# Four quarters of the array for state times q, and GpSimd scatters paced by row tile, in a fused retention and two-layer kernel

## The chip, the cores and the metric

The kernel runs on one NeuronCore of one Trainium2 chip. The metric is device time in microseconds (us), lower is better. The engines are called PE (TensorE, with PEld for its weight loads), DVE (VectorE), ACT (ScalarE), POOL (GpSimd) and SP (SyncE, which issues most transfers). A program line is written L331; the line numbers are those of the kernel before unless the text says otherwise.

## The reference, cut to what matters

Three layers follow each other. Attention with decay (retention) over 8 batches, 8 heads, 576 positions, 64 numbers a head:

```python
scores = q @ k.T / 8
Dmat   = gamma[h] ** (i - j) where i >= j, else 0
x      = (scores * Dmat) @ v            # [4608 tokens, 512]
```

Then a mixture of 8 experts, each token going to the one with the largest logit, and a dense layer with a squared relu:

```python
e = argmax(x @ w_gate + modality_bias[modality_id]);  gate = softmax(...)[e]
x = gate * (relu(x @ w1[e]) @ w2[e])
out = relu(x @ w_in) ** 2 @ w_out
```

All of it is computed in 32-bit floats.

## The kernel before, in words

The program has three stages: retention and routing (to about 232 us of the span), experts (to about 700 us), dense layer (to the end). The change touches the first stage alone.

The first stage walks over 36 row tiles of 128 tokens; nine row tiles hold two batches. For row tile `m` the loop issues, in a fixed order that is written out by hand (each engine takes its instructions in that order):

- `state(m)`: keys times values of the tile are added to a running sum `dps` in PSUM (L312), and ACT copies it, scaled, to `st` (L315).
- `keys(m+1)`, `scores(m+1)`: PE transposes the next tile's keys (`pk`, L278) and DVE scales them (`kj`); PE multiplies keys by queries (`pss`, L290) and DVE masks them to `pm` (L294).
- `outp(m)`: the output of the tile. Eight products of the state with q (L331, the "state products") and eight of v with the masked scores (L334) add up in a PSUM tile `po`. DVE multiplies `po` by a table into `xT` (L342), the transposed rows, which has six buffers.
- `rows_out(m-1)`: PE transposes the rows of the tile before (`pt`, L350), ACT copies them to `xr` and SP writes them to memory as `xl`.
- every fourth tile `logits` (L362, four products side by side in column strips of 32), and then some steps of the routing: the tokens of a group of up to 8 row tiles are ranked by DVE, and each tile gets one scatter on POOL (L447) that writes 128 records of 8 bytes to the table `perm`, each to the row that its rank gives. A one-element memset `spacer` (L446) stands ahead of each scatter.

The heads are taken in pairs: `hp` is the pair (0 to 3), `par` the head in the pair. q, keys and state of a pair lie with head `par` 0 on partitions 0 to 63 and `par` 1 on 64 to 127. A state product contracts over the 64 partitions of its head and writes 64 partitions of `po`, the same half: rows 0 to 63 of the array to columns 0 to 63, or rows 64 to 127 to columns 64 to 127. It is absent in the first tile of a batch pair, and has half as many columns in the tile where the batches meet: 32 tiles have it.

`scatter_some(n)` puts up to `n` scatters that are ready into the program at the end of a row tile: 2 up to tile 28, 4 after it, but none in tiles 27 and 28, where eight gathers (L517) go out for an early expert block. A scatter waits for its ranks only; nothing in it refers to the row tile at whose end it stands, so POOL runs through all scatters of a group once the ranks are there. The records are read back by SP later in the first stage and in the second (`rec`, `recr`).

The pool for `po` has two buffers of one PSUM bank each; with the other pools all eight banks are taken.

Of the kernel before, what the change touches and what calls it, by code (L numbers as in the profile page):

```python
# [5 lines left out]
F32 = mybir.dt.float32  # L6
# [6 lines left out]
A = mybir.AluOpType  # L13
# [5 lines left out]
P = 128  # L19
B, H, S, D = 8, 8, 576, 64  # L20
NT = B * S
DM = H * D
E = 8
# [28 lines left out]
def layouts(inputs):  # L52
# [10 lines left out]
    o["wg"] = np.ascontiguousarray(inputs["moe_w_gate"].reshape(4, P, E).transpose(1, 0, 2))  # L63
    o["mb"] = np.ascontiguousarray(inputs["moe_modality_bias"]).reshape(1, 2 * E)
    o["w1"] = np.ascontiguousarray(inputs["moe_w1"].reshape(E, 4, P, 2, 512).transpose(0, 3, 2, 1, 4).reshape(E, 2, P, 2048))
# [7 lines left out]
def consts():  # L73
# [10 lines left out]
    tabi = gh[:, :, None] ** p.astype(np.float64) / 8.0  # L84
# [33 lines left out]
OPT = dict(manual=True, nbig=10,nlate=10,nx=2,b0=2,bl='SG',rl=2,pz=5,ve=lambda m:'GV' if m<3 or m%4==0 else 'GS',vn=(4,4,2),egn=4,nps=2,npo=2,npt=2,npm=4,nwarm=11,ew=(20,25,32,33),es={23:1,24:1,25:1,26:1,28:1,29:1,30:1,31:1},rlag=2,rlagl=1,rlate=35,rperl=30,e5=5,e6=4,ld=4,rper=8,nw=3,biasat=4,keep=(5,0,4,2),nxw=3,scs=9,e3=11,ylag=2,zlag=2,gb=3,zb=4,cf=(0,6,7,12),cf0=(0,8,9,13),hv=10,zend=1,cwm={0:3},cws={i:(1 if i<4 else 2) for i in range(2,14)},cv0=8,scat=lambda i,n: (2 if i<29 else 4),f3=32,f4=33,e0=dict(ro=1,esplit={2:4,3:2,4:2},r1=0,r2=2,r3=2,tab=(5,6,7,8),rec=4,raw=(0,1,2,3),g1=6,split={5:2,6:2,7:2,8:3,9:3,10:2,11:2},xn1=9,tr0=6,tr1=4),hh=3,hl=3,ylag2=1,bs1=dict(regs=1,rec=1,raw=(3,4,5,6),g0=3,g1=7,gn0=(2,)*4,gn1=(2,)*4,split={6:1,7:1,8:2,9:2,10:1,11:2,12:2,13:1,14:2,15:2},tr0=10,tr1=13,cv=1),bs=dict(regs=-9,rec=-9,raw=(0,3,6,8),g0=-4,g1=4,gn0=(1,)*8,gn1=(1,)*8,split={5:1,6:1,7:2,8:2,9:2,10:2,11:2,12:2,13:2},tr0=5,tr1=13,cv=0,f0=7,p0=13,wm={0:1,3:1,7:1,11:1,13:1},ws={3:2,4:2,5:2,6:2,9:2,10:2}))  # L118


def kernel_body(tc, I, out):
# [199 lines left out]
    def outp(m):  # L321

        t = ins[m]
        r = m % PER
        po = ps_o.tile([P, 4, P], F32, name="po")
        n = C if r == PER // 2 else P
        if r:
            for hp in range(4):
                for par in range(2):
                    rows = slice(D * par, D * par + D)  # L330
                    PE.matmul(po[rows, hp, :n], Ss[m][rows, hp], t.qT[rows, hp, :n], start=(hp == 0), stop=False, skip_group_check=True)  # L331
        for hp in range(4):
            for par in range(2):
                PE.matmul(po[D * par:D * par + D, hp], t.v[:, 2 * hp + par], Ps[m][par][:, hp], start=(r == 0 and hp == 0), stop=(hp == 3), skip_group_check=True)  # L334
# [7 lines left out]
        V.tensor_tensor(out=xT[m].rearrange("p h c i -> p h (c i)"), in0=po, in1=tabi, op=A.mult)  # L342
# [93 lines left out]
    def route3(gi):  # L436
# [15 lines left out]
    scats, soon = [], []  # L452

# [375 lines left out]
    def early_splits(n):  # L829
        for _ in range(n):  # L830
            st.esteps.pop(0)()
# [77 lines left out]
    for m in range(NTILE):  # L909
# [420 lines left out]
```

## Time and profile before

| | |
|---|---|
| timed runs (3) | 1475.81, 1476.97, 1482.99 us; median 1476.97 |
| profiled execution | 1478.18 us, of it the span from first to last instruction 1476.4 |
| PE busy | 1424.2 us (96%) |
| DVE, ACT, POOL busy | 699.5, 458.9, 259.3 us |
| granted TensorE clock, mean | 0.982 |

The span is what the profile divides; 1.8 us lie around it. PE is busy in nearly all of the span, so time that PE stands still, or runs at the lower clock, is read from single stretches. A row of the chronological view gives start, duration, engine, line, operation, out<-in, shapes, count, and in brackets the idle time of the engine just before, with what ended it: a named instruction, "issue" (nothing that the profile shows) or "remote" (a signal whose sender the profile does not find near in time).

### The profile page before, as it was taken

How to read it: one execution, taken by the hardware profiler on the slowest of the kernel's cores; microseconds unless marked ns; L12 is line 12 of the kernel's file. 1: busy time of each engine (PE TensorE's matmuls, PEld its weight loads, DVE VectorE, ACT ScalarE, POOL GpSimd, SP SyncE). 2: the span in 40 equal slices, each digit the busy share in tenths (PEclk: the TensorE clock that was granted, in tenths of full speed). 3: DMA queues.
4: the chain of work that ended last, by engine and by line, in shares of the span. 5: the costliest groups of instructions: out<-in, count | busy, mean ns of one | idle time of the engine just before them, and what ended most of it. 6: DMA issues, size and time to landing. Idle time of an engine off the chain costs nothing.

```text
span 1476.4 us, 21485 instructions
## 1 busy us (share of the span) xinstructions
PE 1424.2 (96%) x8624; PEld 1177.2 (80%) x8624; DVE 699.5 (47%) x1222; ACT 458.9 (31%) x919; POOL 259.3 (18%) x339
## 2 busy tenths in 40 slices
PE   9988797999999999999999999999999999999996
PEld 7776576988888778898888888888888888888885
DVE  5554565778877779746332223222232232223222
ACT  2222133444444344435322222222222222222221
POOL 0112403464534444300001001010010101001010
PEclk9999898999999999999999999999999999999998
DMA  7655555656676666653101001010010101001000
GB/s 262 210 166 187 178 171 149 225 175 200 191 246 206 209 194 196 208 194 138 29 15 34 25 0 57 0 44 15 0 57 1 43 15 43 15 0 43 1 30 15
DMA packets 60250, 154.56 MB, mean 105 GB/s; under 512 B 17004, under 2 KB 27628, under 8 KB 53996
## 3 DMA queue, kind: packets, MB, share of 16 engines
q1 hardware_dynamic: 51436, 133.64, 27.2%
q0 software_dynamic: 8704, 19.45, 4.5%
q8 instruction: 69, 1.13, 0.3%
q14 instruction: 41, 0.34, 0.1%
HBM read 115.73 MB, written 37.34 MB: 104 GB/s over the span
## 4 chain that ended last, share of the span: by engine, by line
PE 44%; issue 8%; POOL 1%; DVE 0%; ACT 0%; POOLq 0%; DVEq 0%; ACTq 0%
PE h L1294 7%; PE h L1293 7%; PE h L1295 7%; PE zp L1250 7%; PE zp L1251 7%; PE zp L1254 7%; POOL out L1265 1%; DVE zo L1263 0%; POOLq L1326 0%; DVE rg L1301 0%; ACT gh L1302 0%; POOL spacer L1264 0%; DVE gl L1303 0%; DVE wlo L492 0%; ACT rg L1300 0%
## 5 line engine op out<-in xcount | busy, mean ns | idle before, releaser
L1301 DVE SCALAR_TENSOR_TENSOR rg<-h,rg 128x512 f32<-128x512 f32 (+1 forms) x159 | 101.6, 639 | 436.4 <-ACT rg L1300 420.1
L1300 ACT ACTIVATE rg<-h 128x512 f32<-128x512 f32 (+1 forms) x159 | 88.2, 555 | 453.8 <-PE h L1295 453.8
L1250 PE MATMUL zp<-whi,gh 128*128 128x512 f32 x576 | 226.5, 393 | 0.5 <-ACT gh L1302 0.4
L1251 PE MATMUL zp<-wlo,gh 128*128 128x512 f32 x576 | 225.9, 392 | 0.0
L1294 PE MATMUL h<-ylo,whi 128*128 128x512 f32 x512 | 201.4, 393 | 0.0
L1293 PE MATMUL h<-yhi,whi 128*128 128x512 f32 x512 | 200.7, 392 | 0.0
L1295 PE MATMUL h<-yhi,wlo 128*128 128x512 f32 x512 | 200.0, 391 | 0.0
L1265 POOL DMA_INDIRECT out<-zo,ti x36 | 34.8, 966 | 807.7 <-ACT zo L1261 665.7
L517 POOL DMA_INDIRECT xg<-xl,rix x136 | 137.9, 1014 | 168.1 <-DVE rix L513 78.8
L1254 PE MATMUL zp<-whi,gl 128*128 128x512 f32 x576 | 162.9, 392 | 0.0
L1303 DVE TENSOR_TENSOR gl<-rg,gh 128x512 fp32r<-128x512 f32 (+1 forms) x160 | 102.2, 639 | 102.9 <-ACT gh L1302 92.7
L1302 ACT CAST gh<-rg 128x512 fp32r<-128x512 f32 (+1 forms) x160 | 92.5, 578 | 119.0 <-DVE rg L1301 119.0
L1254 PEld LDWEIGHTS zp<-whi,gl 128*128 128x128 f32 x576 | 108.1, 188 | 24.9 <-DVE gl L1303 0.2
L1250 PEld LDWEIGHTS zp<-whi,gh 128*128 128x128 f32 x576 | 108.0, 188 | 24.4 <-ACT gh L1302 1.1
L1251 PEld LDWEIGHTS zp<-wlo,gh 128*128 128x128 f32 x576 | 108.3, 188 | 22.6
L607 PE MATMUL yp<-hh,whi 128*128 128x512 f32 (+2 forms) x352 | 123.3, 359 | 0.5 <-DVE yo L620 0.4
L607 PE MATMUL yp<-hh,wlo 128*128 128x512 f32 (+2 forms) x352 | 123.0, 358 | 0.0
L492 DVE TENSOR_TENSOR wlo<-raw,whi 128x512 fp32r<-128x512 f32 x160 | 109.1, 722 | 17.8 <-ACT whi L491 17.3
L1293 PEld LDWEIGHTS h<-yhi,whi 128*128 128x128 f32 x512 | 96.0, 188 | 22.2
L1295 PEld LDWEIGHTS h<-yhi,wlo 128*128 128x128 f32 x512 | 96.2, 188 | 21.7
L1294 PEld LDWEIGHTS h<-ylo,whi 128*128 128x128 f32 x512 | 96.1, 188 | 21.4
L583 PE MATMUL hp<-xlo,whi 128*128 128x512 f32 (+1 forms) x256 | 98.8, 386 | 0.0
(199 smaller groups left out, 2139.3 us busy)
## 6 DMA issues: line engine op xcount, KB each, us to landing
raw<-in_w SPq DMA_DIRECT2D x40, 1024.0 KB
kqv<-in_kqv SPq DMA_DIRECT2D x35, 768.0 KB
xl<-xr SPq DMA_DIRECT2D x34, 256.0 KB
yraw<-yT SPq DMA_DIRECT2D x17, 512.0 KB
craw<-in_wi SPq DMA_DIRECT2D x16, 512.0 KB
cw<-cm SPq DMA_DIRECT2D x32, 256.0 KB
craw<-in_wo SPq DMA_DIRECT2D x16, 512.0 KB
wraw<-cw SPq DMA_DIRECT2D x8, 1024.0 KB
```

Source lines behind the costliest of these rows:

```text
L492: V.tensor_tensor(out=lo[:, j], in0=raws[i][:, j], in1=hi[:, j].bitcast(F32), op=A.subtract)
L517: return lambda: G.indirect_dma_start(out=g.x[:, a].rearrange("p k j -> p (k j)"), out_offset=None, in_=xl.rearrange("t (b e) -> (t b) e", ...
L583: PE.matmul(hp, w1h[:, kc, cs], xlo[:, kc], start=False, stop=False)
L607: PE.matmul(hf.yp[dd], w2[:, fb, dd * P:(dd + 1) * P], h, start=start and f == 0 and (w > HW or dd % 2 == 0), stop=stop and f == 7, skip_g ...
L1250: PE.matmul(zps[s][j], gh[:, cs], wh[:, fb], start=(f == 0), stop=False)
L1251: PE.matmul(zps[s][j], gh[:, cs], wl[:, fb], start=False, stop=False)
L1254: PE.matmul(zps[s][j], gl[:, cs], wh[:, fb], start=False, stop=(f == 15))
L1293: PE.matmul(hp, wh[:, kc, cs], k.hi[:, kc], start=(kc == 0), stop=False)
L1294: PE.matmul(hp, wh[:, kc, cs], k.lo[:, kc], start=False, stop=False)
L1295: PE.matmul(hp, wl[:, kc, cs], k.hi[:, kc], start=False, stop=(kc == 3))
L1301: V.scalar_tensor_tensor(out=g, in0=hp, scalar=0.0, in1=r, op0=A.max, op1=A.mult)
L1303: V.tensor_tensor(out=gl, in0=g, in1=gh.bitcast(F32), op=A.subtract)
```

## The change

Two edits. First, in `outp`, the pairs 2 and 3 of heads write their halves of the output swapped: head `par` 0 (rows 0 to 63 of the array) goes to columns 64 to 127 and head `par` 1 to columns 0 to 63. The state products are issued in the order of pairs 0, 2, 1, 3, so that four in a row stand in four different quarters. `po` becomes two banks wide (pairs 0 and 1 in the first, 2 and 3 in the second, 256 of 512 columns used), and its pool has one buffer in place of two. The tables `tabi`, the gate weights and `w1` are laid out on the host in the matching order of rows.

Second, ahead of each scatter that goes out inside the loop over row tiles, POOL copies one element of the current tile's `xT` into `spacer`, in place of the memset. So the scatter waits until DVE has written `xT` of that tile.

```diff
-OPT = dict(... npo=2 ...)
+OPT = dict(... npo=1 ...)
...
+        gx[:, 2:] = gh[::-1, 2:]
+    tabi = gx[:, :, None] ** p.astype(np.float64) / 8.0
...
-        po = ps_o.tile([P, 4, P], F32, name="po")
+        po = ps_o.tile([P, 2, 512], F32, name="po")
+        def at(hp, par):
+            c = par if hp < 2 else 1 - par
+            return po[D * c:D * c + D, hp // 2, P * (hp % 2):P * (hp % 2) + P]
         if r:
-            for hp in range(4):
+            for hp in (0, 2, 1, 3):
                 for par in range(2):
                     rows = slice(D * par, D * par + D)
-                    PE.matmul(po[rows, hp, :n], Ss[m][rows, hp], t.qT[rows, hp, :n], start=(hp == 0), ...)
+                    PE.matmul(at(hp, par)[:, :n], Ss[m][rows, hp], t.qT[rows, hp, :n], start=(hp % 2 == 0), ...)
...
-        V.tensor_tensor(out=xT[m]..., in0=po, in1=tabi, op=A.mult)
+        V.tensor_tensor(out=xT[m]..., in0=po[:, :, :2 * P], in1=tabi..., op=A.mult)
...
-                G.memset(spacer, 0.0)
+                if pace:
+                    G.tensor_copy(out=spacer, in_=pace[-1])
+                else:
+                    G.memset(spacer, 0.0)
...
+        pace[:] = [xT[m][:, 0, 0, 0:1]]      # at the end of row tile m, before its scatters
...
+    pace.clear()                             # after the last row tile
```

On PE, one row tile before (its state products and what follows up to the next tile's keys); the brackets are the semaphores that a row waits for:

```order
L331 MATMUL po<-kqv,st 64x128 x8
L334 MATMUL po<-pm,kqv 64x128 x8
L350 MATMUL pt<-ident,xT 128x128 [waits DVE_49,Activation_49]
L350 MATMUL pt<-ident,xT 128x128 x3
L312 MATMUL dps<-kqv,kj 64x64 [waits DVE_49,Activation_49]
```

and the same place of the changed kernel, whose lines 343, 346, 362 and 318 are the 331, 334, 350 and 312 of before:

```order
L343 MATMUL po<-kqv,st 64x128 [waits DVE_49]
L343 MATMUL po<-kqv,st 64x128 x7
L346 MATMUL po<-pm,kqv 64x128 x8
L362 MATMUL pt<-ident,xT 128x128 [waits Activation_49]
L362 MATMUL pt<-ident,xT 128x128 x3
L318 MATMUL dps<-kqv,kj 64x64 [waits DVE_49,Activation_49]
```

The number and the place of the products stay; the wait for DVE, which stood at the transposes `pt`, now stands ahead of the first state product, since `po` has one buffer.

On POOL, the start of the first group's scatters before (`pi` are the ranks as whole numbers, `perm` the table):

```order
L445 CAST pi<-pf 128x8 [waits DVE_49]
L446 MEMSET spacer 128x1
L447 DMA perm<-gt,pi 37376x2 [waits DMAHW7_49,Pool_49]
L446 MEMSET spacer 128x1 [waits Pool_49]
L447 DMA perm<-gt,pi 37376x2
L446 MEMSET spacer 128x1 [waits Pool_49]
L447 DMA perm<-gt,pi 37376x2
```

and in the changed kernel (lines 457, 460 and 463 are the 445, 446 and 447 of before):

```order
L457 CAST pi<-pf 128x8 [waits DVE_49]
L460 COPY spacer<-xT 128x1 [waits DVE_49]
L463 DMA perm<-gt,pi 37376x2 [waits DMAHW7_49,Pool_49]
L460 COPY spacer<-xT 128x1 [waits Pool_49]
L463 DMA perm<-gt,pi 37376x2
L460 COPY spacer<-xT 128x1 [waits DVE_49,Pool_49]
L463 DMA perm<-gt,pi 37376x2
```

The order of the scatters is the same; every second one now waits for DVE, the first of each row tile's two. In the third group, which goes out in tiles 29 and 30 four a tile, every fourth one waits.

## Rows read from the trace of the kernel before

**Rows 1.** Busy time of each engine in three stretches, with count, clock, DMA.

```profile
core 0: us, PE busy (x) PEld busy (x) DVE busy (x) ACT busy (x) POOL busy (x), PEclk, DMA share, GB/s
20.00:40.00 20.00, 20.00 (x320) 16.44 (x318) 12.26 (x25) 6.05 (x20) 0.00 (x0) 1.00 0.66 224
66.00:86.00 20.00, 14.95 (x180) 11.61 (x180) 6.09 (x12) 3.02 (x10) 8.87 (x17) 0.83 0.46 129
115.00:135.00 20.00, 15.34 (x177) 10.83 (x178) 7.38 (x21) 3.02 (x10) 8.70 (x17) 0.83 0.38 116
...
600.00:1470.00 870.00, 862.28 (x3973) 716.44 (x3971) 292.25 (x469) 247.20 (x446) 45.09 (x78) 1.00 0.12 41
```

**Rows 2.** POOL in order of time: first and last scatter or gather of three bursts.

```profile
68.22 1.13 POOL L447 DMA_INDIRECT perm<-gt,pi  x1 [0.64 <-POOL spacer L446]
...
77.23 0.96 POOL L447 DMA_INDIRECT perm<-gt,pi  x1 [0.19 <-issue]
...
165.13 1.00 POOL L517 DMA_INDIRECT xg<-xl,rix  x1 [38.25 <-DVE rk L440]
...
184.27 0.95 POOL L447 DMA_INDIRECT perm<-gt,pi  x1 [0.19 <-issue]
...
218.35 0.99 POOL L532 DMA_INDIRECT xg<-xl,rixr  x1 [0.81 <-POOL rixr L525]
...
227.46 0.95 POOL L447 DMA_INDIRECT perm<-gt,pi  x1 [0.19 <-issue]
```

**Rows 3.** PE in order of time, during the first burst.

```profile
69.97 1.09 PE L334 MATMUL po<-pm,kqv 128*64 128x128 f32 x16
...
72.57 0.42 PE L362 MATMUL lg<-xT,wgp 128*32 128x128 f32 x4 [0.25 <-issue]
74.01 0.41 PE L362 MATMUL lg<-xT,wgp 128*32 128x128 f32 x4 [1.02 <-issue]
...
79.75 1.01 PE L312 MATMUL dps<-kqv,kj 64*64 64x64 f32 x14 [0.95 <-issue]
```

**Rows 4.** DVE in order of time: where it writes a tile's rows.

```profile
26.70 0.69 DVE L342 TENSOR_TENSOR xT<-po,tabi_c 128x512 f32<-128x512 f32 x1 [0.72 <-PE po L334]
...
37.15 0.69 DVE L342 TENSOR_TENSOR xT<-po,tabi_c 128x512 f32<-128x512 f32 x1 [0.41 <-PE po L334]
...
65.93 0.69 DVE L342 TENSOR_TENSOR xT<-po,tabi_c 128x512 f32<-128x512 f32 x1 [0.77 <-PE po L334]
...
75.51 0.69 DVE L342 TENSOR_TENSOR xT<-po,tabi_c 128x512 f32<-128x512 f32 x1 [5.17 <-remote]
...
86.00 0.69 DVE L342 TENSOR_TENSOR xT<-po,tabi_c 128x512 f32<-128x512 f32 x1 [0.85 <-PE po L334]
...
164.04 0.68 DVE L342 TENSOR_TENSOR xT<-po,tabi_c 128x512 f32<-128x512 f32 x1
...
194.42 0.69 DVE L342 TENSOR_TENSOR xT<-po,tabi_c 128x512 f32<-128x512 f32 x1 [0.77 <-PE po L334]
...
214.88 0.69 DVE L342 TENSOR_TENSOR xT<-po,tabi_c 128x512 f32<-128x512 f32 x1 [0.35 <-PE po L334]
...
231.83 0.67 DVE L342 TENSOR_TENSOR xlast<-po,tabi_c 128x512 f32<-128x512 f32 x1
```

**Rows 5.** PE in order of time, one undisturbed row tile with logits.

```profile
101.24 1.08 PE L362 MATMUL lg<-xT,wgp 128*32 128x128 f32 x32
102.25 0.66 PE L278 MATMUL pk<-ident,kqv 128*128 128x128 f32 x4
102.84 1.16 PE L290 MATMUL pss<-kqv 64*128 64x128 f32 x16
103.93 1.09 PE L331 MATMUL po<-kqv,st 64*64 64x128 f32 x16
104.95 1.09 PE L334 MATMUL po<-pm,kqv 128*64 128x128 f32 x16
```

**Rows 6.** Groups by line with shapes kept apart: state products.

```profile
L331 PE MATMUL po<-kqv,st 64*64 64x128 f32 x448 | 32.6, 277 | 2.2 <-issue 2.1
...
L331 PE MATMUL po<-kqv,st 64*64 64x64 f32 x64 | 3.2, 247 | 0.0
```

**Rows 7.** Two engines in order of time: the least room of an undisturbed tile.

```profile
156.12 0.68 DVE L342 TENSOR_TENSOR xT<-po,tabi_c 128x512 f32<-128x512 f32 x1
...
157.72 1.09 PE L331 MATMUL po<-kqv,st 64*64 64x128 f32 x16
```

More of the change, by code (lines that the diff above doesn't have):

```diff
@@ L62, in layouts @@
     o["mod"] = np.ascontiguousarray(np.concatenate([four, two], 1))
-    o["wg"] = np.ascontiguousarray(inputs["moe_w_gate"].reshape(4, P, E).transpose(1, 0, 2))
+    dim = np.arange(DM).reshape(4, 2, D)
+    dim[2:] = dim[2:, ::-1].copy()
+    dim = dim.reshape(-1)
+    o["wg"] = np.ascontiguousarray(inputs["moe_w_gate"][dim].reshape(4, P, E).transpose(1, 0, 2))
     o["mb"] = np.ascontiguousarray(inputs["moe_modality_bias"]).reshape(1, 2 * E)
-    o["w1"] = np.ascontiguousarray(inputs["moe_w1"].reshape(E, 4, P, 2, 512).transpose(0, 3, 2, 1, 4).reshape(E, 2, P, 2048))
+    o["w1"] = np.ascontiguousarray(inputs["moe_w1"][:, dim].reshape(E, 4, P, 2, 512).transpose(0, 3, 2, 1, 4).reshape(E, 2, P, 2048))
     o["w2"] = np.ascontiguousarray(inputs["moe_w2"].reshape(E, 2, 4, P, 512).transpose(0, 1, 3, 2, 4).reshape(E, 2, P, 2048))
@@ L83, in consts @@
     tabs = gh[:, None, :] ** first[None, :, None].astype(np.float64)
-    tabi = gh[:, :, None] ** p.astype(np.float64) / 8.0
+    gx = gh.copy()
+    gx[:, 2:] = gh[::-1, 2:]
+    tabi = gx[:, :, None] ** p.astype(np.float64) / 8.0
     upr = (p[:, None] < p[None, :]).astype(np.float32)
@@ L115 @@
     pass
[L118 removed]
+OPT = dict(manual=True, nbig=10,nlate=10,nx=2,b0=2,bl='SG',rl=2,pz=5,ve=lambda m:'GV' if m<3 or m%4==0 else 'GS',vn=(4,4,2),egn=4,nps=2,npo=1,npt=2,npm=4,nwarm=11,ew=(20,25,32,33),es={23:1,24:1,25:1,26:1,28:1,29:1,30:1,31:1},rlag=2,rlagl=1,rlate=35,rperl=30,e5=5,e6=4,ld=4,rper=8,nw=3,biasat=4,keep=(5,0,4,2),nxw=3,scs=9,e3=11,ylag=2,zlag=2,gb=3,zb=4,cf=(0,6,7,12),cf0=(0,8,9,13),hv=10,zend=1,cwm={0:3},cws={i:(1 if i<4 else 2) for i in range(2,14)},cv0=8,scat=lambda i,n: (2 if i<29 else 4),f3=32,f4=33,e0=dict(ro=1,esplit={2:4,3:2,4:2},r1=0,r2=2,r3=2,tab=(5,6,7,8),rec=4,raw=(0,1,2,3),g1=6,split={5:2,6:2,7:2,8:3,9:3,10:2,11:2},xn1=9,tr0=6,tr1=4),hh=3,hl=3,ylag2=1,bs1=dict(regs=1,rec=1,raw=(3,4,5,6),g0=3,g1=7,gn0=(2,)*4,gn1=(2,)*4,split={6:1,7:1,8:2,9:2,10:1,11:2,12:2,13:1,14:2,15:2},tr0=10,tr1=13,cv=1),bs=dict(regs=-9,rec=-9,raw=(0,3,6,8),g0=-4,g1=4,gn0=(1,)*8,gn1=(1,)*8,split={5:1,6:1,7:2,8:2,9:2,10:2,11:2,12:2,13:2},tr0=5,tr1=13,cv=0,f0=7,p0=13,wm={0:1,3:1,7:1,11:1,13:1},ws={3:2,4:2,5:2,6:2,9:2,10:2}))
 def kernel_body(tc, I, out):
@@ L324, in outp @@
         r = m % PER
-        po = ps_o.tile([P, 4, P], F32, name="po")
+        po = ps_o.tile([P, 2, 512], F32, name="po")
         n = C if r == PER // 2 else P
+        def at(hp, par):
+            c = par if hp < 2 else 1 - par
+            return po[D * c:D * c + D, hp // 2, P * (hp % 2):P * (hp % 2) + P]
         if r:
-            for hp in range(4):
+            for hp in (0, 2, 1, 3):
                 for par in range(2):
                     rows = slice(D * par, D * par + D)
-                    PE.matmul(po[rows, hp, :n], Ss[m][rows, hp], t.qT[rows, hp, :n], start=(hp == 0), stop=False, skip_group_check=True)
+                    PE.matmul(at(hp, par)[:, :n], Ss[m][rows, hp], t.qT[rows, hp, :n], start=(hp % 2 == 0), stop=False, skip_group_check=True)
         for hp in range(4):
             for par in range(2):
-                PE.matmul(po[D * par:D * par + D, hp], t.v[:, 2 * hp + par], Ps[m][par][:, hp], start=(r == 0 and hp == 0), stop=(hp == 3), skip_group_check=True)
+                PE.matmul(at(hp, par), t.v[:, 2 * hp + par], Ps[m][par][:, hp], start=(r == 0 and hp % 2 == 0), stop=(hp % 2 == 1), skip_group_check=True)
         if m < NTILE - 2:
@@ L341, in outp @@
             xT[m] = st.xl[:, 512 * (m - NTILE + 2):512 * (m - NTILE + 3)].rearrange("p (h c i) -> p h c i", h=4, c=2)
-        V.tensor_tensor(out=xT[m].rearrange("p h c i -> p h (c i)"), in0=po, in1=tabi, op=A.mult)
+        V.tensor_tensor(out=xT[m].rearrange("p (g h) c i -> p g (h c i)", g=2), in0=po[:, :, :2 * P], in1=tabi.rearrange("p (g h) i -> p g (h i)", g=2), op=A.mult)
     Ls = {}
@@ L452, in kernel_body @@
     scats, soon = [], []
+    pace = []
     def scatter_some(n):
```

## The prediction

> **What bounds the kernel now.** I read the page first (busy time, 40 slices), then busy time by stretch, then the order of time of PE, DVE and POOL where PE fell short. In an undisturbed stretch of the first stage PE is busy for all of 20 us at clock 1.00 while DVE has 12.26 [rows 1]; a row tile's length there is the sum of PE's own steps. After the first two stages PE still fills 862.28 of 870 us [rows 1], so what the first stage saves moves everything behind it forward by as much.
>
> The first stage has holes, and they lie where POOL sends scatters or gathers without a pause. In the first burst eight scatters start from 68.22 to 77.23, one each (77.23 - 68.22) / 7 = 1.29 us [rows 2]. In that stretch PE has 14.95 us of 20 and a mean clock of 0.83 [rows 1], a mix of the two levels 2.4 and 1.2 GHz. PE's rows say how: small packets of products, with gaps of some 1 us put down to "issue", a wait that the profile doesn't name [rows 3]. Signals are late too: the products into `po` end at 69.97 + 1.09 = 71.06, but DVE takes `po` up at 75.51, after 5.17 us idle ended by "remote" [rows 3, 4]. Why a burst does this I can't tell from the rows; that it does, and when, I can. The first gap ends at 72.57 and began 0.25 us sooner, at 72.32: 4.1 us after the first scatter's start. The last ends at 79.75: 1.6 us after the last scatter's end (77.23 + 0.96 = 78.19) [rows 2, 3].
>
> What a burst costs, by the distance between two writes of rows two tiles apart. Undisturbed, with one tile of logits: 37.15 - 26.70 = 10.45. First burst: 86.00 - 65.93 = 20.07, so 9.6 too long. Eight gathers and eight scatters from 165.13 to 184.27: 194.42 - 164.04 = 30.38, 19.9 too long. Two gathers and six scatters from 218.35 to 227.46: 231.83 - 214.88 = 16.95, 6.5 too long [rows 2, 4]. The second group's burst (115 to 135) looks like the first: 15.34 busy, clock 0.83 [rows 1]; I put 9.6. Together 9.6 + 9.6 + 19.9 + 6.5 = 45.6 us.
>
> **The change part by part.** *Scatters paced.* A burst's window of trouble runs from 4.1 us after its start to 1.6 us after its end: for the first, 72.32 to 79.75, or 7.4 us, at a price of 9.6, so 1.3 us per us of window (the slow clock after it is in that).
> - Groups one and two: two scatters a row tile last 1.29 + 0.96 = 2.3 us; with 1.6 after them 3.9, less than 4.1. No window is left, and a tile of some 4.5 us leaves time to recover. That is one end, 0 a pair. The other end is that the price hangs on the scatter and not on the run of them: 9.6 / 4 = 2.4 a pair. I take 0.5, near the end that the first gap's place speaks for. Eight pairs cost 4 (0 to 19.2) in place of 19.2: 15.2 saved.
> - Group three: its eight gathers aren't paced and keep 9.6. Its scatters go out four a tile: 3 x 1.29 + 0.96 + 1.6 - 4.1 = 2.3 us of window, at 1.3 a us 3.0 for each four. New sum 9.6 + 6.0 = 15.6 in place of 19.9: 4.3 saved (0 to 10).
> - Group four: two gathers, unpaced, then four scatters that wait for tile 34 and two for tile 35. The old scatters came up at nearly the same time as that tile's rows, so six still go out in a row: 5 x 1.29 + 0.96 + 1.6 - 4.1 = 4.9 us of window against 7.5 for eight. In proportion to its 6.5 that is 4.2, and 0.5 for the pair: 1.8 saved (0 to 4).
>
> Pacing: 15.2 + 4.3 + 1.8 = 21.3 (0 to 33). The copy that replaces the memset is one element on POOL, idle outside the bursts; what waits behind it is only the next scatter. DVE's write of `xT` six tiles later now also waits for that copy; POOL lags by a few us, six tiles are some 27, so this costs nothing unless POOL hangs back that far. SP reads the records back two tiles or more after the last paced scatter of their groups; a late scatter would hold SP, and the row writes behind it, for a few us, which PE doesn't see as the loads run four tiles ahead. I put nothing.
>
> *State products.* Each product has two records (two passes), 448 / 16 = 28 tiles of full width and 64 / 16 = 4 of half [rows 6]. Now the 16 records go out as 8 pairs, from 103.93 to 104.95, 1.02 us [rows 5]. Four quarters at once make four groups. The trace has no products in four quarters, but it has neighbours on both sides. The logits keep four column strips going: 32 records in eight groups take 102.25 - 101.24 = 1.01, or 0.126 a group. The score products, two row halves at full width, take (103.93 - 102.84) / 8 = 0.136 a pair [rows 5]. Four groups: 0.50 at 0.126, at most 0.71 at 0.136 with 0.17 for changing from one shape to the next (the share of it that is in the averages I leave). Saved 0.31 to 0.52 a tile; I take 0.40: 28 x 0.40 = 11.2, and 0.2 for each of the four half-width tiles, 0.8. Sum 12.0 (9 to 15). PE is what the tile waits for, so this goes to the end in full.
>
> Against this stands a rule. The Trainium skill, "TensorE: Matmul & The Clock Gate", Part 3 on packing small matmuls, says that a weight load overlaps products in flight only when it is for other row groups. The third and fourth products of each four use rows that the first two are using. By that rule pairs would stay pairs, the term be 0 and the time 1457 instead of 1445. The logits speak against it: their four strips share all rows, and a group of four still takes 0.126 us [rows 5]. It is kept below as a rival.
>
> *One buffer for `po`.* PE's wait for DVE moves from the transposes ahead of the state products. DVE writes rows from 156.12 to 156.80, and the next state product starts at 157.72: 0.92 us of room in the tightest undisturbed tile [rows 7]; 65.93 + 0.69 = 66.62 to 68.95 (1.02 ahead of 69.97) is 2.3 in a common one [rows 3, 4]. The steps between the end of `po` and the next state product aren't shortened, so the room stays: 0. DVE's write reads the same 512 numbers a partition from two banks, 0.69 us as now. The second products (L334) still alternate between the column halves, but for one place in the middle where two with the same half follow each other; the two before them use both halves, so nothing is lost. Host layouts cost nothing on the device.
>
> Sum: 1478.2 - 21.3 - 12.0 = 1444.9, say 1445. The profiled execution is 1.2 us above the median of the timed runs, which is less than I can tell.
>
> **The rivals.**
> - *The quarters don't run at once* (rows of the array shared, or two row halves into one PSUM column range hold each other). Pacing alone: 1478.2 - 21.3 = 1457. For: no row shows it working. Against: the logits, and score pairs that write all partitions from two row halves.
> - *The price hangs on the scatter, not on the run.* Pairs and fours then cost as much, spread out: 1478.2 - 12 = 1466. For: `po` is done at 71.06 and DVE learns of it at 75.51, so signals are late before PE has its first gap. Against: PE has no gap in the first 4.1 us.
> - *The single `po` turns late signals into stalls of PE* (slower). After each paced set, DVE would learn late that `po` is done, and PE would stand ahead of the next state products. The place is that wait in the 12 tiles with paced scatters (4 + 4 + 2 + 2). At the delay that the first burst showed, 75.51 - 71.06 = 4.45, less the room of 2.3, it is 2.2 a tile, 26 in all against the 45.6 - 9.6 = 36 that scatters cost now: 1478.2 - 12 - 10 = 1456. It ends slower only from (36 + 12 + 7.4) / 12 = 4.6 us a tile on, twice that.
> - *Nothing changes* (both first rivals): 1478.
>
> **How the numbers follow.** Forecast (both terms work, 1431 to 1453) 0.62; quarters fail, 1457 (1450 to 1466), 0.14; price by scatter, 1466 (1455 to 1472), 0.13; nothing 0.06; slower 0.05. The likeliest time is 1445. Its low end takes 33 for pacing and 15 for the products, 1430; I put 1432. At the top, 1464 takes in the quarters' failure and much of the second rival. A change of 0.5%, 7.4 us, is about what a measurement of this kernel can tell from none; the line lies at 1470. Faster: 0.62 + 0.14 + 0.12 = 0.88; same 0.07; slower 0.05.
>
> **What would show it.** Right: state products some 0.6 us long in a tile of some 4.5; pairs of scatters one tile apart; PE filled and clock 1.00 where the first two bursts were; gaps left at the eight gathers and, shorter, behind the fours. Wrong: gaps of 1 us ended by "issue" after each pair; state products still 1.02 us; idle time of PE ahead of the first state product ended by DVE's `xT`; a clock of 0.5 over more of the stage than now; a new wait at the start of the expert stage that takes back what was gained.

## The result, and the profile after

The changed kernel takes 1453.18 us (median of four runs, 1451.67 to 1460.36), the kernel before beside it 1476.76 (four runs): ratio 0.983, 95% interval [0.981, 0.986]. That is 23.6 us or 1.7% faster; the forecast was 1445 with 1432 to 1464. The profiled execution took 1452.61 us with a span of 1450.8, against 1478.18 and 1476.4 before: 25.6 us less, where the sum of the prediction said 33.3. In the experiments below one run of the kernel before (3674.93 us) and one of the kernel with dead work (2303.38 us) fell far from the others on the same chip, which agree within 11 us; the ratios leave these two out.

Busy time by stretch, with the columns of [rows 1]; the last stretch lies in the expert stage.

```profile
20.00:40.00 20.00, 20.00 (x343) 16.20 (x341) 13.23 (x26) 6.61 (x21) 0.00 (x0) 1.00 0.73 247
66.00:86.00 20.00, 19.55 (x323) 15.55 (x321) 10.95 (x18) 6.06 (x20) 9.44 (x16) 1.00 0.71 180
138.00:158.00 20.00, 15.70 (x182) 10.66 (x180) 8.55 (x26) 3.30 (x12) 7.85 (x10) 0.74 0.57 211
440.00:600.00 160.00, 156.39 (x669) 124.64 (x668) 125.64 (x187) 68.42 (x126) 66.08 (x66) 1.00 0.62 196
```

Where the first burst was, PE now has 19.55 us of 20 at clock 1.00, against 14.95 at 0.83 [rows 1]. The hole that is left in the first stage is the one at the unpaced gathers (138 to 158): 15.70 at 0.74.

PE in order of time, in an undisturbed tile; it answers to [rows 5].

```profile
58.20 1.16 PE L296 MATMUL pss<-kqv 64*128 64x128 f32 x16
59.30 0.67 PE L343 MATMUL po<-kqv,st 64*64 64x128 f32 x16
59.89 1.09 PE L346 MATMUL po<-pm,kqv 128*64 128x128 f32 x16
```

The state products (now L343) last from 59.30 to 59.89, 0.59 us in place of 1.02.

DVE in order of time, where it writes a tile's rows (now L354); it answers to [rows 4].

```profile
56.54 0.69 DVE L354 TENSOR_TENSOR xT<-po,tabi_c 128x512 f32<-128x512 f32 x1 [0.36 <-PE po L346]
61.04 0.69 DVE L354 TENSOR_TENSOR xT<-po,tabi_c 128x512 f32<-128x512 f32 x1 [0.36 <-PE po L346]
...
71.49 0.68 DVE L354 TENSOR_TENSOR xT<-po,tabi_c 128x512 f32<-128x512 f32 x1
...
81.36 0.69 DVE L354 TENSOR_TENSOR xT<-po,tabi_c 128x512 f32<-128x512 f32 x1 [0.28 <-PE po L346]
...
137.11 0.68 DVE L354 TENSOR_TENSOR xT<-po,tabi_c 128x512 f32<-128x512 f32 x1
150.40 0.69 DVE L354 TENSOR_TENSOR xT<-po,tabi_c 128x512 f32<-128x512 f32 x1 [7.38 <-remote]
...
173.78 0.69 DVE L354 TENSOR_TENSOR xT<-po,tabi_c 128x512 f32<-128x512 f32 x1
...
184.53 0.69 DVE L354 TENSOR_TENSOR xT<-po,tabi_c 128x512 f32<-128x512 f32 x1
...
197.22 0.66 DVE L354 TENSOR_TENSOR xlast<-po,tabi_c 128x512 f32<-128x512 f32 x1
```

A tile without scatters is 61.04 - 56.54 = 4.50 us, before 4.92 or 4.93. Across the first burst's place the two tiles from 61.04 to 71.49 take 10.45, before 20.07. At the gathers one tile still takes 150.40 - 137.11 = 13.29, with 7.38 us of DVE waiting for a late signal ("remote").

The row of tile 35 comes at 197.22 in place of 231.83 [rows 4]: 34.6 us ahead, about what was forecast for the whole program. Nine of these are gone by the end. PE in order of time at three places where they go: in the early expert block, later in the expert stage, and on entering the dense stage:

```profile
204.55 0.17 PE L444 MATMUL pr_all<-ohf,uprb 128*128 128x16 bf16 x1 [3.26 <-DVE ohf L418]
...
465.09 0.50 PE L624 MATMUL yp<-hl,whi 128*128 128x512 f32 x1 [1.40 <-DVE hl L605]
...
637.32 0.36 PE L1312 MATMUL pr_all<-yhl,whi 128*128 128x256 f32 x1 [0.93 <-PEq L1235]
...
640.26 0.39 PE L1312 MATMUL pr_all<-yhl,whi 128*128 128x256 f32 x1 [2.34 <-issue]
```

To see where a lead is won and lost, the start of the same DVE row is subtracted between two traces: rows of `xT` by tile, and in the expert stage rows of `hl` (the low half of an expert's hidden numbers; there are 88 such rows) by their count. Lead over the kernel before, in us:

| trace | tile 27 | tile 31 | tile 35 | 9th hl | 49th hl | 81st hl | end |
|---|---|---|---|---|---|---|---|
| changed kernel | 26.9 | 31.2 | 34.6 | 32.3 | 32.0 | 28.9 | 25.6 |
| quarters alone | 9.5 | 9.8 | 11.9 | 13.0 | 9.7 | 8.4 | 5.4 |
| pacing alone | 20.0 | 26.7 | 34.2 | 31.8 | 31.0 | 30.8 | 29.2 |
| changed, one meta transfer | 23.3 | 28.7 | 32.0 | 31.9 | 31.2 | 33.8 | 32.0 |
| changed, gathers paced too | 26.7 | 43.5 | 47.5 | 40.1 | 35.6 | 32.7 | 29.4 |

The four lower rows are experiments, below; one profile each, where the kernels' own runs spread by up to 14 us. A second profile of the kernel before itself differs from the first by up to 2.8 us in these columns, so smaller differences in the table say nothing.

### The profile page after: what moved, and what is told of

It is laid out like the page before. It is cut to its first block, busy times and chain, and to the rows that moved or that the text cites. A ratio compares the mean times of both kernels' runs of the same rounds, so it can differ in the third digit from the quotient of the medians.

```text
span 1450.8 us, 21479 instructions
## 1 busy us (share of the span) xinstructions
PE 1409.4 (97%) x8624; PEld 1165.2 (80%) x8624; DVE 698.1 (48%) x1222; ACT 459.0 (32%) x919; POOL 263.4 (18%) x339
## 3 DMA queue, kind: packets, MB, share of 16 engines
HBM read 115.73 MB, written 37.34 MB: 106 GB/s over the span
## 4 chain that ended last, share of the span: by engine, by line
PE 52%; issue 3%; POOL 0%; POOLq 0%; DVE 0%; ACT 0%; ACTq 0%
PE h L1313 9%; PE h L1312 9%; PE h L1314 9%; PE zp L1269 9%; PE zp L1270 9%; PE zp L1273 9%; POOL out L1284 0%; POOLq L1345 0%; PE pr_all L1312 0%; PE pr_all L1314 0%; PE pr_all L1313 0%; DVE gl L1322 0%; DVE rg L1320 0%; ACT gh L1321 0%; ACT rg L1319 0%
## 5 line engine op out<-in xcount | busy, mean ns | idle before, releaser
L1284 POOL DMA_INDIRECT out<-zo,ti x36 | 34.6, 962 | 810.7 <-ACT zo L1280 665.7
L1270 PEld LDWEIGHTS zp<-wlo,gh 128*128 128x128 f32 x576 | 108.3, 188 | 22.6
L509 DVE TENSOR_TENSOR wlo<-raw,whi 128x512 fp32r<-128x512 f32 x160 | 108.2, 715 | 21.8 <-ACT whi L508 21.3
L1312 PEld LDWEIGHTS h<-yhi,whi 128*128 128x128 f32 x512 | 96.0, 188 | 22.2
```

The costliest lines, as they stand in the source:

```text
L509: V.tensor_tensor(out=lo[:, j], in0=raws[i][:, j], in1=hi[:, j].bitcast(F32), op=A.subtract)
L1270: PE.matmul(zps[s][j], gh[:, cs], wl[:, fb], start=False, stop=False)
L1312: PE.matmul(hp, wh[:, kc, cs], k.hi[:, kc], start=(kc == 0), stop=False)
```

## The experiments

Twelve experiments ran on three chips, on each with runs of the kernel before between them. The kernel before took 1479.88 us (13 runs) on the first, **1430.02 (26 runs) on the second**, 1479.44 (13) on the third: the second chip is 49 us faster with the same program. So ratios are compared (microseconds saved are worked out from them), and the second chip is read by itself.

**Quarters alone** (first chip). The paced copy is left out; the old memset stands ahead of each scatter.

```diff
-        pace[:] = [xT[m][:, 0, 0, 0:1]]
```

> The changed kernel with the old memset ahead of every scatter, so that scatters go out in bursts again; the state products stay in four quarters and po in one buffer. Theory (two separate terms): the state products phase stays near 0.59 us and a tile without scatters near 4.50 us, the first two bursts cost their 9 to 10 us each again, and the first stage gives 28 x 0.42 + 4 x 0.2 = 12.6 us: 1464 us. If the single po made a burst dearer, it would be above 1470. Rival (the products gain nothing of themselves and only pacing pays): 1477. If the expert stage takes back a share of any gain (it took 6.5 of 32 in the changed kernel), 1466 to 1468.

Ratio 0.9957 [0.9942, 0.9972], 6.4 us less. The bursts are back, in its DVE rows:

```profile
61.37 0.69 DVE L354 TENSOR_TENSOR xT<-po,tabi_c 128x512 f32<-128x512 f32 x1 [0.36 <-PE po L346]
...
81.40 0.69 DVE L354 TENSOR_TENSOR xT<-po,tabi_c 128x512 f32<-128x512 f32 x1 [1.27 <-PE po L346]
```

Two tiles take 81.40 - 61.37 = 20.03, of 9.8 undisturbed (the 10.45 of before less the 0.64 that the products save in a full tile and one with half the columns). That is 10.2 for the burst, against 9.6 with two buffers, so in an unpaced burst the single `po` costs 0.6, less than two profiles of the kernel before differ there (20.07 and 18.87). The products bring their 12 us by tile 35 (11.9 in the table), as forecast, and half of it is lost behind. The time, 1473.56, misses the 1464 of the theory and the 1466 to 1468 with a loss behind it.

**Pacing alone** (first chip, and again on the third). The kernel before with these lines:

```diff
-                G.memset(spacer, 0.0)
+                if pace:
+                    G.tensor_copy(out=spacer, in_=pace[-1])
+                else:
+                    G.memset(spacer, 0.0)
...
+        pace[:] = [xT[m][:, 0, 0, 0:1]]
...
```

> The kernel before with the paced scatters alone: state products in pairs, po in two buffers. Theory (two terms, and a fixed loss behind them): at the start of the expert stage some 36.5 - 13.4 = 23 us ahead of the kernel before, of which 4 are lost at once to the scatters of the last groups, which follow each other without a pause, and 0 to 6.5 later in the expert stage: 1457 to 1464. Rival (the expert stage can take only so much, and gives back whatever comes above it): the lead at 640 us is 25 or so, and the time nearly that of the changed kernel, 1453. Rival (pacing is worth only what my prediction's lower bound said): 1477.

Ratio 0.9867 [0.9839, 0.9895], 19.7 us less; on the third chip 0.9846 [0.9818, 0.9874], 22.8. It is the least steady of the kernels: its four runs lie between 1448.96 and 1463.28, and the profile in the table is the fastest of them. At the end the two halves, 6.4 + 19.7 = 26.1, add up to about the changed kernel's gain (23.6, and 29.9 on the third chip).

At tile 35 they do not add up: pacing alone is 34.2 us ahead there, quarters alone 11.9, both together 34.6. Up to tile 27 they still do, nearly (20.0, 9.5 and 26.9). DVE's rows of tiles 27, 29, 33 and 35 in this kernel, and the busy time of tiles 29 to 33, here and in the changed kernel:

```profile
144.07 0.68 DVE L342 TENSOR_TENSOR xT<-po,tabi_c 128x512 f32<-128x512 f32 x1
...
164.34 0.69 DVE L342 TENSOR_TENSOR xT<-po,tabi_c 128x512 f32<-128x512 f32 x1 [0.84 <-PE po L334]
...
187.90 0.69 DVE L342 TENSOR_TENSOR xT<-po,tabi_c 128x512 f32<-128x512 f32 x1 [0.24 <-PE po L334]
...
197.63 0.69 DVE L342 TENSOR_TENSOR xlast<-po,tabi_c 128x512 f32<-128x512 f32 x1 [1.49 <-PE pt L350]
```

```profile
164.34:187.90 23.56, 21.81 (x353) 17.47 (x353) 17.50 (x37) 8.42 (x25) 9.72 (x16) 1.00 0.55 153
```

```profile
157.23:184.53 27.30, 24.29 (x353) 18.98 (x353) 17.82 (x36) 8.31 (x25) 9.69 (x16) 0.81 0.43 123
```

From tile 27 to 35 pacing alone takes 197.63 - 144.07 = 53.56, the changed kernel 197.22 - 137.11 = 60.11, though its products should save 3.2 there: 9.7 too long. On the third chip the same sum gives 59.26 - 52.24 + 3.2 = 10.2. Nearly all of it lies behind tile 29, at the two fours of group three and at group four. For the same 353 records PE's mean clock is 0.81 from tile 29 to 33, and it stands three times ahead of `po` products (0.46, 0.57 and 0.62 us, put down to "issue"); pacing alone keeps a clock of 1.00 and has no such gap. So of the 12 us that the products bring by themselves in the first stage, some 10 are lost again when the scatters are paced. The order of the products is not what does it: with the other one (on the third chip, below) the stretch takes 57.41, still 8.3 too long. Whether it is the quarters or the single buffer of `po`, no run separates.

**One transfer for meta** (first chip). An expert slot writes two small tables of records; the second write stood in SP's queue until the first had landed.

```diff
+        if len(hs) == 2 and dst.shape[0] == 2 * HW:
+            nc.sync.dma_start(out=dst.rearrange("(h i a) w -> i h (a w)", h=2, a=8), in_=rec[:HW // 8].rearrange("p h a w -> p h (a w)"))
+            return
```

> The changed kernel with the two small writes of an expert slot's records (meta) sent as one transfer, so that SP no longer stands between them until the first has landed, with the loads of the next weights queued behind. Theory (SP's queue makes the weights late): SP's wait for meta, 34 us in seven places, goes; the weights' loads are issued some 5 us sooner; PE's waits ahead of yp between 440 and 640 us shrink; the lead of 32 us that the stage loses there (6.5) comes back in part: 1447 to 1451. Rival (the rate of the transfers, or DVE's and ACT's queues, set the pace there): 1453 as now. The first stage does not change and shows how well a profile repeats.

Ratio 0.9778 [0.9759, 0.9797]. SP's rows of one such place, before, in the changed kernel and in this one:

```profile
501.87 6.68 SPq L627 DMA_DIRECT2D meta<-rec  x2
```

```profile
470.70 6.83 SPq L644 DMA_DIRECT2D meta<-rec  x2
```

```profile
468.81 0.45 SPq L643 DMA_DIRECT2D meta<-rec  x1
```

Waits of SP and of ACT by releaser in the changed kernel, 440 to 600 us (us in total, times, longest):

```profile
SPq L644 <- DMA meta<-rec: 12.3, 2, 6.4
...
ACT cm L795 <- DMA cw<-cm: 25.5, 8, 5.4
...
ACT whi L508 <- DMA raw<-in_w: 15.5, 4, 4.6
```

ACT's waits in this kernel over the same 160 us:

```profile
ACT cm L798 <- DMA cw<-cm: 3.1, 6, 1.2
ACT whi L508 <- DMA raw<-in_w: 2.5, 3, 1.3
```

Its busy time, from 4 us sooner:

```profile
436.00:596.00 160.00, 160.00 (x697) 130.58 (x696) 128.63 (x191) 69.10 (x125) 67.82 (x66) 1.00 0.62 199
```

SP's wait is gone; the loads of weights and the writes behind it come in time; ACT hardly waits for them, and PE is busy for all of 160 us in place of 156.39. The table shows it as a lead that grows from 31.2 to 33.8 where the changed kernel's falls from 32.0 to 28.9. This names one of the places where the gain went, and a price for it: 3.6 us by PE's busy time, 5.7 by the leads. The kernel with all edits, on the second chip, repeats it: PE 157.00 of 157 us there, against 154.57 in the kernel with fours.

**Gathers paced, in threes** (first chip). The copy goes ahead of the eight early gathers too, three a tile, and the third group's scatters follow three and four a tile.

```diff
-scat=lambda i,n: (2 if i<29 else 4)
+scat=lambda i,n: (2 if i<29 else 3 if i<31 else 4)
...
-            gather_some(st.exs, o_.egn)
+            for _ in range(min(3, len(st.exs.steps))):
+                G.tensor_copy(out=spacer, in_=pace[-1])
+                gather_some(st.exs, 1)
+            if not st.exs.steps:
+                scatter_some(1)
```

> The changed kernel with the eight early gathers paced as well, and the third group's scatters with them: three a row tile over tiles 27 to 30 and four in tile 31, in place of eight gathers without a pause and two times four scatters. By the window rule of the prediction (trouble from 4.1 us after the first to 1.6 us after the last, 1.3 us of cost a us) three cost 1.4 us and four 3.0: 4 x 1.4 + 3.0 = 8.4 in place of some 9.6 + 6, so 6 to 7 us less by the end of the first stage; 1446 to 1448 if it stays. Rival (the price is by the transfer, not by the run): no gain, 1453. Rival (the expert stage takes it back): the lead at 200 us grows by 6 and the time stays at 1451 to 1453.

Ratio 0.9791 [0.9758, 0.9824]. Tiles 27, 31 and 33, by its DVE rows:

```profile
137.33 0.68 DVE L354 TENSOR_TENSOR xT<-po,tabi_c 128x512 f32<-128x512 f32 x1
...
161.45 0.68 DVE L354 TENSOR_TENSOR xT<-po,tabi_c 128x512 f32<-128x512 f32 x1
...
174.67 0.69 DVE L354 TENSOR_TENSOR xT<-po,tabi_c 128x512 f32<-128x512 f32 x1 [0.73 <-PE po L346]
```

Up to tile 31 it takes 24.12 us in place of 173.78 - 137.11 = 36.67. But only twelve of the sixteen transfers lie in it: the last four go out from 162.95 on, and tiles 31 to 33 take 13.22 here, 10.75 in the changed kernel. Both together are 37.34 in place of 47.42: 10.1 less, where the window rule said 6 to 7. By tile 35 the lead is 47.5, 13 more than the changed kernel's. At the end 4 of these 13 are left. In the early expert block the fourth and fifth groups' scatters follow each other without a pause (PE 12.17 busy of the 20 us from 180, clock 0.76), and the lead falls from 47.5 to 40.1; the rest goes in the expert stage.

**Second chip.** Four variants, all of the changed kernel. First, the fifth group's scatters are held for the early expert's hidden rows:

```diff
-    scatter_some(9)
+    scatter_some(2)
...
+        if hf is ek and f < 4:
+            pace[:] = [hl[:, 0:1].bitcast(F32)]
...
-        scatter_some(o_.scs)
+        scatter_some(2)
```

> The changed kernel with the fifth group's four scatters held back as well: two wait for the first early hl, two for the next, in place of four directly behind the fourth group's. Theory (the run of twelve scatters from 188 to 206 us makes the 3.3 us gap of PE ahead of the last routing product and the slow clock there): the gap shrinks to under 1.5 us and the first hl's of the early expert come 2 to 4 us sooner; 1449 to 1451 if the rest of the stage keeps it. Rival (the start of the first slot hangs on the chain scatter, records, gather, xn, not on PE): the gap ahead of tr at 220 grows by what the other shrinks, lead at 236 us still 32, 1453.

Then everything that had helped, together with that, and the fourth group's scatters not held:

```diff
-        pace[:] = [xT[m][:, 0, 0, 0:1]]
+        pace[:] = [xT[m][:, 0, 0, 0:1]] if m < NTILE - 2 else []
```

> Everything that helped in one kernel: the changed kernel with gathers and scatters of tiles 27 to 31 paced in threes, the fourth group's scatters not held for tile 34, the fifth group's held for the early expert's hl, and one transfer for meta. Theory (the losses are separate): threes were worth 4.9 at the end and one meta transfer 6.5 by the medians; together 1453 - 11 = 1442, with the expert stage's head perhaps 1439. Rival (the expert stage takes only so much lead): lead at 286 us no more than 36, and 1445 to 1447.

Then dead work on PE:

```diff
+        if m == 6:
+            for _ in range(40):
+                warmup()
```

> The changed kernel with forty warm-up products (128 x 512, bf16, each 0.21 us) ahead of tile 7's work: about 8.6 us of PE time that do nothing, in the undisturbed part of the first stage. Theory (what the first stage gains or loses is passed on only in part, because the weights' loads set the pace at the start and from 440 us on): all of it arrives at tile 11, but less than 8.6 at the end, 4 to 7: 1457 to 1460. Rival (my prediction's step: the first stage moves everything by as much): 1461.8.

Last, four scatters a tile in the first two groups:

```diff
-scat=lambda i,n: (2 if i<29 else 4)
+scat=lambda i,n: 4
```

> The changed kernel with the first two groups' scatters four a row tile in place of two (two tiles of four in place of four tiles of two). By the window rule of the prediction a four costs 3.0, so 2 x 3.0 a group in place of 4 x 0.5 or less: 8 more for both groups, 1461. Rival (price by the scatter): no change, 1453. Rival (the price starts only with a longer run, as the fours of the third group cost more only because they follow the gathers): under 1 us each, 1454.

Ratios, in this order: 0.9969 [0.9957, 0.9982], 0.9951 [0.9933, 0.9969], 1.0002 [0.9988, 1.0016], 0.9967 [0.9954, 0.9980]. None of the expected times could come, since the kernel before took 49 us less on this chip; the traces show where. The kernel with fours sends its gathers and the third group's scatters as the changed kernel does. Its first two groups come out as eight scatters in a row (from 67.33 to 77.77 in the first), since the rows that the second four wait for are written by then. POOL in order of time, the first gather and the last scatter of sixteen:

```profile
138.84 1.00 POOL L534 DMA_INDIRECT xg<-xl,rix  x1 [24.28 <-DVE rk L452]
...
159.26 0.96 POOL L463 DMA_INDIRECT perm<-gt,pi  x1 [0.16 <-issue]
```

Its busy time where the first burst and the gathers stand:

```profile
66.00:86.00 20.00, 20.00 (x356) 16.07 (x353) 11.40 (x18) 6.65 (x21) 9.48 (x16) 1.00 0.68 141
...
138.00:158.00 20.00, 20.00 (x368) 16.21 (x367) 16.27 (x45) 7.53 (x23) 15.59 (x23) 1.00 0.87 274
```

DVE's rows of tiles 11 and 15, and 27 and 31:

```profile
60.95 0.69 DVE L354 TENSOR_TENSOR xT<-po,tabi_c 128x512 f32<-128x512 f32 x1 [0.36 <-PE po L346]
...
80.02 0.69 DVE L354 TENSOR_TENSOR xT<-po,tabi_c 128x512 f32<-128x512 f32 x1 [0.28 <-PE po L346]
...
137.75 0.68 DVE L354 TENSOR_TENSOR xT<-po,tabi_c 128x512 f32<-128x512 f32 x1
...
158.54 0.69 DVE L354 TENSOR_TENSOR xT<-po,tabi_c 128x512 f32<-128x512 f32 x1 [0.35 <-PE dps L318]
```

Sixteen transfers leave POOL in 21 us without a pause, and PE is busy for 20.00 of 20 us at clock 1.00, where the changed kernel had 15.70 at 0.74 (above). The kernel with dead work, which keeps two scatters a tile, takes the same 19.06 us for the four tiles that the eight in a row take here (80.02 - 60.95). **On this chip a burst costs nothing.** So the fours couldn't be priced (window or no window, both are 0 there), and pacing has nothing to save. What would be left of the change is the products, and the ratio of the two variants nearest to it (0.9967, 0.9969: 4.4 to 4.7 us) is near that of the quarters alone (0.9957). The changed kernel itself did not run on this chip, and the kernel before left no trace there.

The dead work was 8.6 us: in its trace tile 7's row lies 9.5 behind that of the kernel with fours, tile 6's 0.9. By the medians it ends 1430.13 - 1425.3 = 4.8 behind the kernel with fours, which stands in for the changed one. The first theory expected 4 to 7, but this does not show it. The two profiles are 8.6 apart at the end (that of the fours is the fastest of its ten runs), and 11.0 at the 81st `hl`: 2.4 is won back behind it, mostly on entering the dense stage, where this kernel lacks a gap that the other has (below). So the experiment leaves open how much the expert stage passes on.

Holding the fifth group did not help. PE's row ahead of the first slot, in that kernel and in the one with fours:

```profile
198.07 1.33 PE L565 MATMUL tr<-ident,xn 128*128 128x128 f32 x5 [6.81 <-DVE xn L555]
```

```profile
196.28 0.98 PE L565 MATMUL tr<-ident,xn 128*128 128x128 f32 x7 [3.31 <-DVE xn L555]
```

The wait for `xn` (scatters, then the records read back, then the gathered rows) grew by 3.5, as the rival said. The 3.26 us gap that it was made for doesn't occur in these traces, so what makes that gap was not tested.

**Third chip.** The kernel before and the changed one again, for their traces, and the state products in another order:

> The kernel before itself, for its trace on the chip of this call. In the call just made the kernel before took 1430 us, against 1477 to 1480 in the two calls ahead of it, and there a run of eight scatters (the fours) left no gap in PE. Theory (what a run of scatters costs belongs to the chip): where the kernel takes about 1430, PE has no gaps of 1 us at the bursts of 68 to 78 and 165 to 184 us, signals there come in time, and two writes of xT across the first burst lie 10.5 us apart, as in an undisturbed stretch, not 20; where it takes about 1478, the trace is that of before. Rival (the bursts cost the same everywhere, and the 47 us come from elsewhere in the program): gaps and 20 us there as well, and the difference in another stage.

> The changed kernel itself on the same chip. Theory (two terms, one of them the chip's): where bursts cost nothing, pacing gives nothing, the products give their 12 us at tile 35 and the expert stage keeps about half of it, as with the quarters alone (6.3 by the medians): 1424, ratio 0.996. Where bursts cost as on the first chip: 1453, ratio 0.983. Rival (the paced copies themselves cost or gain): another ratio than that of the quarters alone where bursts are free.

> The kernel before with the paced scatters alone, on the same chip. Theory: where bursts cost nothing, 1430, ratio 1.000 within 0.2%. Where they cost as on the first chip, 1457, ratio 0.987. Rival (waiting scatters make the records late and hold the start of the expert stage): slower than before by 2 or more where bursts cost nothing.

```diff
-            for hp in (0, 2, 1, 3):
+            for hp in range(4):
```

> The changed kernel with the state products in the order of the four head pairs 0, 1, 2, 3 in place of 0, 2, 1, 3: every product stays in its quarter, but only the neighbours 1 and 2 are then pairs for different quarters. Theory (products for different quarters run at once only when they follow each other in the queue): 7 groups of the 8 pair times are left: the phase takes 0.85 to 0.95 us in place of 0.59, and a tile 4.75 to 4.85 in place of 4.50; about 8 to 10 us later than the changed kernel at tile 35. Rival (the place alone decides, the engine takes them together in any order): 0.59 and 4.50. Rival (the skill's rule, a weight load waits for products on its rows): no state product overlaps beyond its pair, 1.02 and 4.92, in both orders, which the trace of the changed kernel has already spoken against.

This chip is like the first. Two rows of the kernel before across its first burst:

```profile
65.92 0.69 DVE L342 TENSOR_TENSOR xT<-po,tabi_c 128x512 f32<-128x512 f32 x1 [0.77 <-PE po L334]
...
84.79 0.69 DVE L342 TENSOR_TENSOR xT<-po,tabi_c 128x512 f32<-128x512 f32 x1 [0.36 <-PE po L334]
```

It took 1479.60, two tiles across the burst 84.79 - 65.92 = 18.87; the changed kernel 1450.14, ratio 0.9798 [0.9776, 0.9819]; pacing alone as told above. Against this trace of before the changed kernel leads by 31.3 at tile 35 and 25.7 at the end, which repeats the first table row; pacing alone by 32.5 and 24.0.

The order gave 1446.54, ratio 0.9769 [0.9741, 0.9798], no slower than the changed kernel. PE in order of time:

```profile
54.94 0.68 PE L343 MATMUL po<-kqv,st 64*64 64x128 f32 x16
55.55 1.09 PE L346 MATMUL po<-pm,kqv 128*64 128x128 f32 x16
```

0.61 us, not 0.85 to 0.95: my theory fell; in these two orders the place alone decides. Products that stand eight records further down the program, for the other two quarters, still run beside the first ones: in that order sixteen records would take nearly the 1.02 us of two quarters if they did not.

## Why the prediction was right, and where it was not

**The first stage as a whole was sized well.** The price of each place can now be measured: four tiles of the changed kernel's work without any trouble take 80.02 - 60.95 = 19.07 on the second chip, and 3 x 0.42 + 0.22 = 1.48 more with the products in pairs (one tile of the four has half the columns). In the same way for the other places, in us of trouble. The first number of a difference is the distance between DVE's rows of tiles 11 and 15, 19 and 23, 27 and 31, 33 and 35, the second that of the second chip.

| place | before, forecast | before, measured | after, forecast | after, measured |
|---|---|---|---|---|
| group one | 9.6 | 29.91 - 20.55 = 9.4 | 2.0 | 20.32 - 19.07 = 1.3 |
| group two | 9.6 | 29.94 - 20.47 = 9.5 | 2.0 | 19.49 - 18.99 = 0.5 |
| gathers and group three | 19.9 | 40.93 - 22.27 = 18.7 | 15.6 | 36.67 - 20.79 = 15.9 |
| group four | 6.5 | 16.95 - 8.62 = 8.3 | 4.7 | 12.69 - 7.78 = 4.9 |

Trouble before 45.9 (forecast 45.6), after 22.6 (24.3), saved 23.3 against the 21.3 of the sum. Before's 46 us are nearly the 49 us by which the second chip is faster. Group four was forecast too low (6.5 for 8.3), because the prediction took off 10.45, the length of two other tiles; these two take 8.62 undisturbed.

**Its two terms were not, and that they came out together is in part luck.** The prediction added a saving by pacing (21.3) and one by the products (12.0). Pacing alone is worth 34.2 us at tile 35 (32.5 on the third chip), 13 more than its term: with pairs and two buffers the gathers and fours cost 34.19 - 22.27 = 11.9 from tile 27 to 31, and group four 9.73 - 8.62 = 1.1, against 15.9 and 4.9 in the changed kernel. Beside it the products add 0.4 us by then (on the third chip they take 1.2 away). The forecast had no term by which one edit makes the other dearer.

**State products.** 0.42 a full tile, 0.22 a half one: 28 x 0.42 + 4 x 0.22 = 12.6 where nothing else disturbs them, forecast 12.0. The first rival is out: the Trainium skill, "TensorE: Matmul & The Clock Gate", Part 3, lets weight loads overlap only across row groups, which would have left 1.02 us; the trace has 0.59, and 0.61 in the other order, and the measurement decides.

**Price by the run, not by the scatter.** Eight pairs cost 1.8 us together (1.3 + 0.5) where the same sixteen scatters in bursts cost 18.9, so the second rival is out too. The window rule itself is only rough. For the kernel with threes it gave 8.4, and they cost 24.12 - 20.79 = 3.3 up to tile 31 (twelve transfers) and 13.22 - 9.32 = 3.9 up to tile 33 (the last four). For gathers and fours it gave 15.6, and they cost 15.9 and 10.75 - 9.32 = 1.4 in the changed kernel, but 11.9 with pacing alone.

**The single `po`** cost 0.6 at most in unpaced bursts, and no stall of PE at paced pairs: in the changed kernel PE misses 0.45 of the 20 us from 66. There the third rival is out. At the paced fours and in group four it is not: the some 10 us told above are lost there, PE idles ahead of `po` products, and the single `po` is one of the two things that differ from pacing alone and could do it. Its sign, idle time ahead of the first state product ended by DVE's `xT`, is not seen, as the profile puts this idle time down to "issue". The cause stays open.

**The other step that failed** is the first paragraph's: "what the first stage saves moves everything behind it forward by as much", and with it "this goes to the end in full". It rested on PE's 862.28 busy us of 870 from 600 on [rows 1]; the stretch between, the expert stage, wasn't read. In it the lead of 34.6 shrank to 25.6: 2.3 in the early expert block, 0.3 to the 49th hl, 3.1 to the 81st, 3.3 from there through the entry to the dense stage.
- The early block: the last scatters, held back by the pacing, now follow each other nearly without a pause from 188 to 206 us, and PE waits 3.26 us for the last routing product. The place is seen; that the scatters are its cause was not shown. The kernel with one meta transfer, with the same first stage, has no such gap (none above 0.7 us) and loses nothing there. Pacing alone lost 2.4 in one profile and 10.3 on the third chip (32.5 to 22.2).
- From 440 to 600 us: SP stands between two small writes, weights come late, ACT and then PE wait. Shown by the single transfer, which takes these waits away. Before has the same wait (6.68, 6.69 and 6.54 us in order of time, in the changed kernel 6.83, 7.67 and 6.48) and lost 1.4 us there (155.64 busy of the 157 us from 475). That the changed kernel loses more is not due to its shorter first stage. DVE's rows from the 49th to the 81st `hl` take 179.5 to 179.8 us in the four traces with pairs, among them both of pacing alone, which come there 24 and 31 us ahead; 180.8 to 182.7 in the eight with quarters and two writes, on all three chips and with the smallest lead too; and 176.9 to 177.0 in the two with one write. So it goes with the quarters; why stays open.
- The entry to the dense stage, just behind a branch (L1235): gaps of 0.93 and 2.34 us and then a clock of 0.66 from 640 to 645. The kernel before has gaps of 0.70, 1.07 and 0.42 there. Eight of the nine other traces with the quarters have the large gap of 2.2 to 2.5 as well; the traces with pairs don't, and neither does the kernel with dead work, whose PE code is forty products longer. One thing more goes with it in all fourteen traces: the queue q8, which brings the program's code in blocks of 16 KB, fetches two blocks behind this entry, the second about 4 us after it and so behind the gap, in the nine with the large gap, and one alone in the five without. Its line in the profile's view of DMA for 5 us from the entry on, in the changed kernel (637 to 642) and before (664.5 to 669.5):

```profile
q8 instruction: 2, 0.03, 3.2%
```

```profile
q8 instruction: 1, 0.02, 1.3%
```

So the gap seems to go with where the program's code lies and not with what is computed; the fetch itself was not varied.

By the ratios the products thus gave 6 to 7 us at the end (quarters alone 6.4; changed kernel less pacing alone 29.9 - 22.8 = 7.1, uncertain by some 5) of the 12.0, and pacing 19.7 to 22.8. That this is the 21.3 of the forecast is luck: it is 34 in the first stage less what is lost behind. With the products taken at 6 to 7 the sum would have been 1450 to 1451, near the measured 1453.18 and 1450.14, for the same lucky reason.

**What the forecast could not see**: the larger term belongs to the chip, or to its condition. On the second one bursts cost 0, and the two variants nearest to the change save 0.3%, about what the products do alone.

No version was clearly the best. Where bursts cost, the one meta transfer (0.9778), the threes (0.9791) and the other order (0.9769) lie together, below the changed kernel's first measurement (0.983), but their intervals overlap that of its second (0.9798); all edits together ran only on the second chip, 0.9951.

## What to carry to other kernels

Read each stage between the edit and the end before a gain is passed on in full: a stage whose PE is 98% busy can still be paced by a queue, and a gain can stay there in part. Measure two edits each alone and together, at the end of the stage that they touch: a sum that fits can hide two terms that don't. Where one engine's signals are late only during runs of GpSimd transfers, break the runs, to two or three a few microseconds apart, the gathers as much as the scatters; and measure the kernel before on more than one chip, since such a price may be that of the chip. Two small writes of which the second waits for the first hold everything behind them in their queue: send them as one.

## What the runs showed of the hardware

- The same program took 1430 us on one chip (26 runs) and 1479 to 1480 on two others (13 runs each). On the fast one a run of sixteen GpSimd transfers in 21 us left PE at 20.00 busy us of 20; on the others a run of eight cost 8 to 10 us, with PE's clock at 0.83 in the 20 us around it and DVE waiting 5.2 us for a late signal (7.4 at eight gathers). Each chip was used once, so whether it is the chip or its condition at that time is open.
- Where bursts cost, three indirect transfers a tile cost far less than eight in a row: 3.3 us for twelve in threes and 7.2 with a four behind them, 17.3 for eight gathers and two fours, 18.7 for all sixteen in a row.
- Four 64 x 64 quarters run sixteen records in 0.59 us where two quarters took 1.02, and 0.61 when all records of two quarters are queued ahead of those of the others: products later in the program start beside earlier ones.
